# A gated feed-forward layer behind a spectral mixer: side work given out step by step between products

## The chip, the cores and the metric

The kernel runs on one core of one Trainium2 chip. The metric is the device time of one execution, in microseconds. Before the change three runs took 1896.96, 1904.18 and 1904.19 us; their median is 1904.18 us.

The engines have short names in the profile: PE is the matrix engine (PEld its weight loads), DVE the vector engine, ACT the scalar engine, POOL the general-purpose engine, SP the engine that issues most transfers. Each takes its instructions in the order in which the program gave them out, and waits at an instruction until what it needs is there.

## The reference

All is float32. There are 4096 positions of 640 channels. The first half normalises them, takes a real Fourier transform over the positions, passes the frequencies through two block-diagonal layers with a soft threshold, transforms back and adds the result to `x`. The second half normalises again and adds a gated feed-forward layer of 1728 hidden channels. Six vectors that come from `c` scale, shift and gate the two halves.

```python
mod = (_silu(c) @ w_mod).reshape(c.shape[0], 6, 1, -1)
sa, ca, ga, sb, cb, gb = ...
h = _layernorm(x) * (1 + ca) + sa
x = x + ga * _A_ref(h, A_w1, A_b1, A_w2, A_b2)      # spectral mixer
h = _layernorm(x) * (1 + cb) + sb
x = x + gb * ((_silu(h @ w_gate) * (h @ w_up)) @ w_down)
```

## The kernel before

The mixer fills the first 329 us and is not touched. The change lies in the second half, which runs from there to the end.

**Precision.** A float32 operand is split into a rounded high part and a low part, the rest (ACT copies the high part, DVE subtracts for the low part). A product is then three matmuls: high by high, high by low, low by high.

**Tiles.** The positions are 32 rows of 128. `TL` (L922) cuts them into six tiles t = 0 to 5 with 4, 6, 6, 6, 6 and 4 rows. Each tile goes through the same list of stages `STG`: `g0 u0 s g1 d0 u1 g2 d1 u2 g3 d2 u3 g4 d3 u4 g5 d4 u5 m d5`. A stage g, u or m multiplies the tile by 256 columns of the gate weights, of the up weights, or of 128 of both; s takes the last 64 columns of both. A stage d multiplies 256 hidden channels by the down weights and adds the result to `x`; d5 takes the rest of the hidden channels too.

- Tile 0 multiplies plainly (`plain`, L1293: 30 matmuls of 512 columns in a stage).
- Tiles 1 to 5 multiply two by two blocks with seven products in place of eight (`seven`, L1333: 54 matmuls of 384 columns, of 256 in tile 5). Four PSUM banks X, Y, Z, V gather the products. ACT copies a bank to SBUF at four moments (`keep`, L1360, tiles s_x, s_v, s_y, s_z), and the bank is then added to further. PE may go on in a bank when its copy is done. `done` (L1366) adds a bank to a copy (DVE), and makes SiLU (stage g) or multiplies by the gate and splits the result (stage u, m).
- `down` (L1435): 6 matmuls of 320 columns for each half of each row, and an addition on DVE.

**Side work.** Beside its products a tile has other work, done by ACT, DVE, POOL and SP, partly by PE:

- weights: load (`load_w`, L997), split (`prep_w`, L1017); in tile 0 also the block sums T1 to T4 of the seven products (`sum_w`, L1041: four POOL subtractions, two splits), which are stored to DRAM (`td`) and loaded again in each later tile (`load_t`, L1008). The place for them has two buffers, one for each half;
- down weights: load (`load_wd`), multiply by the gate vector on POOL (`fold_wd`, L1089), split (`split_wd`);
- the rows of the next tile: load (`row_load`), split (L1142, L1143), the last step of the inverse transform on PE (`row_dft`, L1152), residual and statistics on DVE, two small POOL steps, the normalised row (`row_norm`, L1164); for a pair of rows ten transposes on PE (`pair_turn`, L1177), scale and shift on ACT, four block sums on POOL, four splits, stores to DRAM (`hs`). The next tile loads all its pairs with `load_h` (L1228) at its start.

**The order around the change.** The program writes out the order by hand. `row_steps(t)` puts each of the row steps into a numbered stage: some at the stage's start, ahead of its products (the transform and the transposes), the others into a list `todo` with the weight steps. `fill()` is called six times in a stage and gives out a sixth of `todo`; the rest follows at the stage's end. Transfers for the next stages (`load_w`, `load_t`) are begun at the stage's start.

Of the kernel before, what the change touches and what calls it, by code (L numbers as in the profile page):

```python
# [171 lines left out]
def body(tc, x, w1, b1, w2, b2, wg, wu, wd, c, wm, k_fa, k_tb, k_tx, k_bm, k_bx, k_ga, k_ge, k_id, out, dbg=None):  # L172
# [27 lines left out]
    with ExitStack() as top:  # L200
# [716 lines left out]
        with ExitStack() as ff:  # L917
# [69 lines left out]
            def any_bank(name):  # L987
                nxt[0] += 1
                return bank((0, 1, 2, 3)[nxt[0] % 4], name)
# [7 lines left out]
            def load_w(t, n):  # L997
                k, p = WG[n]
                r = take("R", [P, 5, 256], F32, 2, f"r{t}_{n}")
# [8 lines left out]
            def load_t(t, n):  # L1008
                if WG[n][0] == "s":
                    return  # L1010
                for i in range(2):
                    wt = take("wt", [P, 2, 2, 2, P], F32R, 2, f"wt{t}_{n}{i}")
                    nc.sync.dma_start(f32(wt.rearrange("p a b c d -> p (a b c d)")), td[n, i])
                    wts[t, n, i] = wt


            def prep_w(t, n):  # L1017
# [12 lines left out]
                for ks in (slice(0, 2), slice(2, 5)):  # L1030
                    out += [lambda ks=ks: high(ks), lambda ks=ks: low(ks)]
                if c == P and t:

                    e, ks = slice(P, 2 * P), slice(0, 2)
                    out.insert(0, lambda: pool.tensor_tensor(r[:, ks, e], r[:, 1:4:2, 0:P], r[:, 0:4:2, 0:P],  # L1035
                                                             op=OP.subtract))
                    out += [lambda: high(ks, e), lambda: low(ks, e)]
# [3 lines left out]
            def sum_w(n):  # L1041
                r = raw[0, n]
                if WG[n][0] == "s":
                    return []
                ts = take(f"h{6 * (n % 2)}", [P, 4, 2, P], F32, 1, f"ts{n}")
# [3 lines left out]
                def sub(o, a, b):  # L1049
                    return lambda: pool.tensor_tensor(ts[:, o], a, b, op=OP.subtract)  # L1050

                out = [sub(3, b12, b11), sub(1, b22, ts[:, 3]), sub(0, b22, b12), sub(2, b21, ts[:, 1])]
                for i in range(2):
                    wt = take("wt", [P, 2, 2, 2, P], F32R, 2, f"wt0_{n}{i}")
                    wts[0, n, i] = wt
                    src = ts[:, 2 * i:2 * i + 2]

                    def high(wt=wt, src=src):
                        act.activation(wt[:, :, 0], src, AF.Copy)

                    def low(wt=wt, src=src):
                        dve.tensor_tensor(wt[:, :, 1], src, f32(wt[:, :, 0]), op=OP.subtract)

                    out += [high, low]
                return out

            def store_t(n):
                for i in range(2):
                    if (0, n, i) in wts:
                        nc.sync.dma_start(td[n, i], f32(wts[0, n, i].rearrange("p a b c d -> p (a b c d)")))  # L1070
# [3 lines left out]
            wds = {}  # L1074

# [10 lines left out]
            def fold_wd(t, p):  # L1086
                w = wdraw[t, p]
                for f in range(2):
                    pool.tensor_tensor(w[:, f], w[:, f], gbb, op=OP.mult)  # L1089

            def split_wd(t, p):
                w = wdraw[t, p]
                h = take("wdh", [P, 2, D], F32R, 2, f"wdh{t}_{p}")
                l = take("wdl", [P, 2, D], F32R, 2, f"wdl{t}_{p}")
                wds[t, p] = (h, l)
                out = []
                for f in range(2):
                    out += [lambda f=f: act.activation(h[:, f], w[:, f], AF.Copy),  # L1098
                            lambda f=f: dve.tensor_tensor(l[:, f], w[:, f], f32(h[:, f]), op=OP.subtract)]  # L1099
                return out  # L1100
# [15 lines left out]
            def gate_sum():  # L1116
                for hf in range(2):
                    pm = any_bank(f"gpm{hf}")
# [10 lines left out]
            hp_ = {}  # L1129

            def row_load(r):
# [3 lines left out]
                nc.sync.dma_start(crs[r], s2[:, r, :])  # L1135
                gtr[r] = fp.tile([P, 2, N1], F32R, tag="gt", bufs=2, name=f"gt{r}")
                pool.dma_start(gtr[r].rearrange("p b c -> p (b c)"), k_ga[:, 256 * r:256 * r + 256])

            def row_split(r):
                chh = take("pc", [P, D], F32R, 4, f"chh{r}")  # L1140
                chl = take("pc", [P, D], F32R, 4, f"chl{r}")
                act.activation(chh, crs[r], AF.Copy)  # L1142
                dve.tensor_tensor(chl, crs[r], f32(chh), op=OP.subtract)  # L1143
                chs[r] = (chh, chl)

            def row_dft(r):
                x2, gt = xr[r], gtr[r]
                chh, chl = chs[r]
                for hf in range(2):
                    e = slice(320 * hf, 320 * hf + 320)  # L1150
                    py = any_bank(f"py{r}_{hf}")
                    mm(py[:, :320], gt[:, 0, :], chh[:, e], start=True, stop=False)  # L1152
                    mm(py[:, :320], gt[:, 0, :], chl[:, e], start=False, stop=False)
                    mm(py[:, :320], gt[:, 1, :], chh[:, e], start=False, stop=True)
                    yg = take("s", [P, 320], F32, 5, f"yg{r}_{hf}")
                    dve.tensor_tensor(yg, py[:, :320], gab[:, e], op=OP.mult)
                    dve.tensor_tensor(x2[:, e], x2[:, e], yg, op=OP.add)
                mvs[r] = layer_stats(fp, x2.unsqueeze(1), 1, f"b{r}")

            def row_norm(r):  # L1160
                nc.sync.dma_start(x2d[:, r, :], xr[r])
                mv, rs = mvs[r]
                xn[r] = take("pc", [P, D], F32, 4, f"xn{r}")
                dve.tensor_scalar(xn[r], xr[r], mv[:, 0, 0:1], rs[:, 0:1], op0=OP.subtract, op1=OP.mult)  # L1164


            def pair_turn(t, i):
                r0, H = TL[t]
                rows = (r0 + i, r0 + H + i)
                h32 = take("h32", [P, 5, 2, P], F32, 1, f"h32_{t}_{i}")  # L1170
                hp_[t, i] = h32
                for q in range(3):
                    pt = any_bank(f"pt{t}_{i}_{q}")
                    for k in range(2 * q, min(2 * q + 2, 5)):
                        for a in range(2):
                            c = 256 * (k % 2) + 128 * a
                            pe.transpose(pt[:, c:c + 128], xn[rows[a]][:, 128 * k:128 * k + 128], idn)  # L1177
                    for k in range(2 * q, min(2 * q + 2, 5)):
                        c = 256 * (k % 2)
                        act.activation(h32[:, k].rearrange("p a b -> p (a b)"), pt[:, c:c + 256], AF.Identity,  # L1180
                                       bias=sb1[:, k:k + 1], scale=cb1[:, k:k + 1])


            def pair_parts(t, i):
                h32 = hp_[t, i]
                A = [[h32[:, b:4:2, a] for b in range(2)] for a in range(2)]
                sa_ = take("pc", [P, 2, 2, P], F32, 4, f"sa{t}_{i}")
                sb_ = take("pc", [P, 2, 2, P], F32, 4, f"sb{t}_{i}")
                S1, S2, S3, S4 = sa_[:, 0], sa_[:, 1], sb_[:, 0], sb_[:, 1]
                out = []  # L1190

                def tt(o, a, b, op):
                    return lambda: pool.tensor_tensor(o, a, b, op=op)

                out += [tt(S1, A[1][0], A[1][1], OP.add), tt(S3, A[0][0], A[1][0], OP.subtract),
                        tt(S2, S1, A[0][0], OP.subtract), tt(S4, A[0][1], S2, OP.subtract)]
                pieces = [[A[0][0], A[0][1]], [A[1][1], h32[:, 4]], [S1, S2], [S3, S4]]
                for j, src in enumerate(pieces):
                    ho = {}

                    def high(j=j, src=src, ho=ho):
                        o = fp.tile([P, 2, 2, 2, P], F32R, tag="ho", bufs=2, name=f"ho{t}_{i}_{j}")
                        ho[0] = o
                        for b in range(2):
                            act.activation(o[:, b, :, 0], src[b], AF.Copy)

                    def low(j=j, src=src, ho=ho):
                        o = ho[0]
                        for b in range(2):
                            dve.tensor_tensor(o[:, b, :, 1], src[b], f32(o[:, b, :, 0]), op=OP.subtract)  # L1210

                    def store(j=j, ho=ho):
                        nc.sync.dma_start(
                            hsd[t][:, 2 * j:2 * j + 2, :, :, 128 * i:128 * i + 128].rearrange(
                                "p a b c d -> p (a b c) d"),
                            f32(ho[0].rearrange("p a b c d -> p (a b c) d")))

# [400 lines left out]
```

## Time and profile before

| what | us |
|---|---|
| median of three runs | 1904.18 |
| profiled execution, its own time | 1901.75 |
| its span | 1900.0 |
| mixer, before the second half's first transposes | 329 |
| tile 0, to the start of d5; its d5 | 214.0; 28.8 |
| tile 1 | 298.1 |
| tile 2 | 286.7 |
| tile 3 | 286.0 |
| tile 4 | 265.7 |
| tile 5 | 191.7 |

The tiles are cut at the first matmul of their first stage. In a window's row the profile gives the time in which each engine was busy and, as PEclk, the share of full speed that the chip granted PE's clock. A row of waits reads: the waiting engine, what it was about to do, what it waited for, the sum in us, how often, the longest.

### The profile page before, as it was taken

To read this page: it belongs to the slowest core of one execution; us is meant where nothing else is said; L and a number is where in the kernel's file an instruction comes from. 1 tells how busy PE (TensorE), PEld (TensorE's weight loads), DVE (VectorE), ACT (ScalarE), POOL (GpSimd) and SP (SyncE) were. 2 spreads that over 40 slices of the span, in tenths; PEclk is the share of its full clock that TensorE was granted. 3 is DMA by queue.
4 is the path that set the end of the run, shared out by engine and by line. 5 is a ranking of instruction groups with operands and counts; after the bars stand their busy time and mean duration, and the time that the engine had idled before them with its cause. 6 is when DMAs were issued, how large, how long until landed. Compare 5 with 4: busy or idle time off the path is not lost.

```text
span 1900.0 us, 24357 instructions
## 1 busy us (share of the span) xinstructions
PE 1545.8 (81%) x8939; PEld 1443.1 (76%) x8939; DVE 1179.3 (62%) x2165; ACT 778.6 (41%) x1578; POOL 349.3 (18%) x433
## 2 busy tenths in 40 slices
PE   7699999777675877888877888877889788887778
PEld 3599997566565877788867888767879788887777
DVE  8578887656552665664665664665664666654665
ACT  7589884524232333342332342333342343323332
POOL 4301003344231021121021121021121021200111
PEclk9899999998887888999888999988899899999999
DMA  9745554635556563557553557553557545455442
GB/s 383 275 145 171 179 178 153 223 132 175 192 171 251 177 188 105 174 158 272 173 175 110 163 169 261 189 157 123 164 165 259 197 138 167 153 196 180 168 147 90
DMA packets 206680, 344.29 MB, mean 181 GB/s; under 512 B 20640, under 2 KB 136544, under 8 KB 204512
## 3 DMA queue, kind: packets, MB, share of 16 engines
q1 hardware_dynamic: 198336, 325.85, 51.7%
q0 software_dynamic: 6928, 14.91, 2.5%
q10 hardware_dynamic: 1296, 1.97, 0.3%
q8 instruction: 70, 1.15, 0.2%
q14 instruction: 50, 0.41, 0.1%
HBM read 249.88 MB, written 83.62 MB: 176 GB/s over the span
## 4 chain that ended last, share of the span: by engine, by line
PE 43%; DVE 22%; ACT 14%; DMA 10%; issue 6%; POOL 3%; SPq 2%; ACTq 0%; DVEq 0%; POOLq 0%
PE pd L1466 17%; PE pw L1350 5%; PE pw L1352 4%; PE pw L1351 4%; DVE wb L1028 4%; DVE sg L1380 3%; ACT a L1282 2%; DVE wdl L1099 2%; DVE a L1283 2%; DMA wdr<-in_B_w_down_dram 2%; ACT wb L1025 2%; PE pc L649 2%; DMA wt<-td 2%; DMA h<-hs 1%; DVE chl L1143 1%
## 5 line engine op out<-in xcount | busy, mean ns | idle before, releaser
L1466 PE MATMUL pd<-wdh,a 128*128 128x320 f32 x1712 | 398.5, 316 | 14.9 <-ACT wdh L1098 14.1
L1089 POOL TENSOR_TENSOR wdr<-wdr,gbb 128x640 f32<-128x640 f32 x84 | 142.1, 1710 | 1001.8 <-DMA wdr<-in_B_w_down_dram 751.0
L1466 PEld LDWEIGHTS pd<-wdh,a 128*128 128x128 f32 x1712 | 298.8, 194 | 16.5 <-ACT wdh L1098 15.1
L1350 PE MATMUL pw<-h,wt 128*128 128x384 f32 (+1 forms) x520 | 185.2, 356 | 119.1 <-ACT s_y L1362 68.6
L1466 PE MATMUL pd<-wdl,a 128*128 128x320 f32 x888 | 279.9, 316 | 2.5 <-DVE wdl L1099 2.1
L1028 DVE TENSOR_TENSOR wb<-r,wb 128x512 fp32r<-128x512 f32 (+3 forms) x173 | 160.4, 937 | 190.3 <-ACT wb L1025 183.4
L1470 DVE TENSOR_TENSOR x<-x,pd 128x320 f32<-128x320 f32 x384 | 180.7, 485 | 139.3 <-PE pd L1466 138.0
L1350 PEld LDWEIGHTS pw<-h,wt 128*128 128x128 f32 x520 | 104.7, 201 | 137.6 <-ACT s_y L1362 82.1
L1352 PE MATMUL pw<-h,wt 128*128 128x384 f32 (+1 forms) x520 | 177.5, 341 | 0.0
L1351 PE MATMUL pw<-h,wt 128*128 128x384 f32 (+1 forms) x520 | 177.0, 340 | 0.0
L1466 PEld LDWEIGHTS pd<-wdl,a 128*128 128x128 f32 x888 | 171.9, 194 | 5.6 <-DVE wdl L1099 5.5
L1362 ACT ACTIVATE s_x<-pw 128x384 f32<-128x384 f32 (+1 forms) x65 | 30.2, 465 | 328.0 <-PE pw L1352 328.0
L1282 ACT ACTIVATE a<-sg 128x384 fp32r<-128x384 f32 (+2 forms) x142 | 72.8, 512 | 216.8 <-DVE sg L1380 195.0
L1283 DVE TENSOR_TENSOR a<-sg,a 128x384 fp32r<-128x384 f32 (+2 forms) x142 | 93.7, 660 | 95.6 <-ACT a L1282 95.6
L1350 PE MATMUL pw<-h,wb 128*128 128x384 f32 (+1 forms) x390 | 140.2, 359 | 12.7 <-ACT wb L1025 11.9
L1352 PE MATMUL pw<-h,wb 128*128 128x384 f32 (+1 forms) x390 | 138.8, 356 | 2.7 <-DVE wb L1028 2.1
L1351 PE MATMUL pw<-h,wb 128*128 128x384 f32 (+1 forms) x390 | 137.2, 352 | 0.0
L1025 ACT ACTIVATE wb<-r 128x512 fp32r<-128x512 f32 (+3 forms) x173 | 115.5, 704 | 38.1 <-POOL r L1035 18.0
L1099 DVE TENSOR_TENSOR wdl<-wdr,wdh 128x640 fp32r<-128x640 f32 x84 | 70.2, 848 | 74.5 <-ACT wdh L1098 74.4
L1351 PEld LDWEIGHTS pw<-h,wt 128*128 128x128 f32 x520 | 105.3, 203 | 0.0
L1352 PEld LDWEIGHTS pw<-h,wt 128*128 128x128 f32 x520 | 104.5, 201 | 0.0
L1356 PE MATMUL pw<-h,wb 128*128 128x384 f32 (+1 forms) x260 | 88.5, 340 | 8.2 <-ACT s_z L1362 8.2
(252 smaller groups left out, 3331.0 us busy)
## 6 DMA issues: line engine op xcount, KB each, us to landing
wt<-td SPq DMA_DIRECT2D x130, 512.0 KB, 3.7
hs<-ho SPq DMA_DIRECT2D x56, 512.0 KB, 4.2
h<-hs SPq DMA_DIRECT2D x32, 768.0 KB, 11.3
r<-in_B_w_gate_dram SPq DMA_DIRECT2D x36, 640.0 KB, 6.0
r<-in_B_w_up_dram SPq DMA_DIRECT2D x36, 640.0 KB, 5.7
wdr<-in_B_w_down_dram SPq DMA_DIRECT2D x36, 640.0 KB, 5.7
td<-wt SPq DMA_DIRECT2D x25, 512.0 KB, 4.3
g<-s SPq DMA_DIRECT2D x28, 320.0 KB, 7.1
```

What stands on the lines that cost most here:

```text
L1025: act.activation(wb[:, 0, ks, e], r[:, ks, e], AF.Copy)
L1028: dve.tensor_tensor(wb[:, 1, ks, e], r[:, ks, e], f32(wb[:, 0, ks, e]), op=OP.subtract)
L1089: pool.tensor_tensor(w[:, f], w[:, f], gbb, op=OP.mult)
L1099: lambda f=f: dve.tensor_tensor(l[:, f], w[:, f], f32(h[:, f]), op=OP.subtract)]
L1282: act.activation(hi, a32, AF.Copy)
L1283: dve.tensor_tensor(lo, a32, f32(hi), op=OP.subtract)
L1350: mm(b, w(0, kp), a[:, kp, 0], start=start and kp == 0, stop=False, skip_group_check=not start)
L1351: mm(b, w(0, kp), a[:, kp, 1], start=False, stop=False, skip_group_check=not start)
L1352: mm(b, w(1, kp), a[:, kp, 0], start=False, stop=kp == 1, skip_group_check=not start)
L1356: mm(b, wb[:, 0, 4, c], AK[:, half, 0], start=False, stop=False, skip_group_check=True)
L1466: mm(pd[g, hf][:, :320], l, m, start=(i == 0), stop=(i == len(q) - 1))
L1470: dve.tensor_tensor(x2[:, e], x2[:, e], pd[g, hf][:, :320], op=OP.add)
```

## The change

The list `todo` and the numbered stages go. In their place stand six chains of single steps: `gate`, `prep` (weights), `down_w` (down weights), `sums`, `parts` (block sums of tile 0 and their splits) and `rows`. A step has an engine, a length in us, a function that gives out its instructions, and a pause until the next. The program keeps a count `now` of the time of PE's products and a count `free` for each engine. Every few matmuls it calls `slot`, which gives out those steps whose chain is due and whose engine is free by these counts; products' own work on ACT and DVE is added to the counts by `core`. Chains are emptied (`flush`) where their result is needed: `prep` at the end of a stage, `down_w` at the stage d that needs it, `rows` at d5.

Other edits: in `seven` the copies of the banks come first on ACT, the SiLU or high part of a quadrant follows after the next copy, the low part after that. `load_t` is called for each half where PE has given out the last product that reads the half's place, in place of both at the stage's start. In tile 0 weights are loaded three stages ahead, with a third buffer in a place (`h1`) that is empty until tile 1; g0's block sums and weights of tile 1 are fetched ahead of d5 instead of after it. Banks for side products are taken from three of the four bank names.

Each engine is given the same number of instructions by both kernels (PE 8672, DVE 2167, ACT 1589, POOL 438, SP 711); the order alone is another.

```diff
+            class Chain:
+                def add(self, steps, start=0.0):
+                    if not self.steps:
+                        self.ready = max(self.ready, now[0] + start)
+                    self.steps += steps
+                def run(self):
+                    e, n, f, pause = self.steps.pop(0)
+                    f()
+                    if e == "T":
+                        now[0] += n
+                        free[e] = now[0]
+                    else:
+                        free[e] = max(free[e], now[0]) + n
+                    self.ready = free[e] + pause
...
+            gate, prep, down_w, sums, parts, rows = chains = [Chain() for _ in range(6)]
+            def slot(n, hold=""):
+                now[0] += n
+                for c in chains:
+                    while c.steps and c.ready <= now[0] and free[c.steps[0][0]] <= now[0] + 0.2:
+                        if c.steps[0][0] in hold:
+                            break
+                        c.run()
...
+                return ([("A", 0.75, high, 0.1), ("V", 0.82, low, 0.3)],
+                        [("T", 0.45, lambda: dft(0), 0.0), ("T", 0.45, lambda: dft(1), 0.0),
+                         ("V", 1.0, lambda: residual(0), 0.0), ("V", 1.0, lambda: residual(1), 0.0),
+                         ("V", 1.2, stats, 0.1), ("S", 0.5, store, 1.4), ("V", 0.6, norm, 0.2)])
...
                 prod(V, S3, "T3", True)
                 s7 = keep(V, "v")
-                fill()
+                slot(2 * u)
                 prod(Y, A12, "B21", True)
                 fifth(Y, 0, 0)
-                fill()
-                done(0, 0, Y, s1)
+                summed(0, 0, Y, s1)
+                slot(1.5 * u)
+                slot(1.5 * u)
                 prod(X, S2, "T2")
-                s2_ = keep(X, "y")
-                fill()
+                sy = keep(X, "y")
+                high(0, 0, s1)
+                at(0)
+                slot(2 * u)
                 prod(V, A22, "T4")
                 fifth(V, 1, 0)
+                low(0, 0)
+                summed(1, 0, V, sy)
...
+                    if what == "d":
+                        while (t, NPR if n == NPR - 1 else n) not in wd_done:
+                            down_w.run()
+                        if n == NPR - 1:
+                            rows.flush()
+                            if t == 0:
+                                sums.flush()
+                                parts.flush()
+                                for i in range(2):
+                                    load_t(1, 0, i)
+                                prep.add(prep_w(1, 0))
+                            if t + 1 < NT:
+                                load_h(t + 1)
+                        down(t, n)
...
+                    if n == 2:
+                        if t == 0:
+                            prep_wd(0, 0)
+                            prep_wd(0, 1)
+                        else:
+                            load_x2(t)
+                        if t + 1 < NT:
+                            row_chain(t + 1)
```

More of the change, by code (lines that the diff above doesn't have):

```diff
@@ L1049, in sub @@
                 def sub(o, a, b):
[L1050 to L1070, printed above, removed]
+                    def f():
+                        if not ts:
+                            ts.append(take(f"h{6 * (n % 2)}", [P, 4, 2, P], F32, 1, f"ts{n}"))
+                        pool.tensor_tensor(ts[0][:, o], a if a is not None else ts[0][:, 3],
+                                           b if not isinstance(b, int) else ts[0][:, b], op=OP.subtract)
@@ L1176, in pair_turn @@
                             c = 256 * (k % 2) + 128 * a
-                            pe.transpose(pt[:, c:c + 128], xn[rows[a]][:, 128 * k:128 * k + 128], idn)
-                    for k in range(2 * q, min(2 * q + 2, 5)):
[L1179 to L1216, printed above, removed]
-                    out += [high, low, store]
-                return out
@@ new lines, in low, with store @@
+                def low(j):
+                    for b in range(2):
+                        dve.tensor_tensor(ho[j][:, b, :, 1], src(j)[b], f32(ho[j][:, b, :, 0]), op=OP.subtract)
+                def store(j):
+                    nc.sync.dma_start(
+                        hsd[t][:, 2 * j:2 * j + 2, :, :, 128 * i:128 * i + 128].rearrange("p a b c d -> p (a b c) d"),
+                        f32(ho[j].rearrange("p a b c d -> p (a b c) d")))
+                out = []
+                for q in range(3):
+                    out.append(("T", 0.1 * (4 if q < 2 else 2), lambda q=q: turn(q), 0.2))
+                    for k in range(2 * q, min(2 * q + 2, 5)):
+                        out.append(("A", 0.4, lambda k=k: scale(k), 0.0))
@@ L1221, in body, with pair_steps_at @@
+            def pair_steps_at(t, i, more):
+                st = pair_steps(t, i)
+                n = next(k for k, q in enumerate(st) if q[0] == "P")
+                return st[:n + 2] + more + st[n + 2:]
             hb = {}
@@ L1297, in plain @@
                     pg = first_g()
+                    for _ in range(8):
+                        slot(0.85)
                 else:
@@ L1400, in seven @@
-                fill()
+                sz = keep(X, "z")
+                high(1, 0, sy)
+                at(1)
+                slot(2 * u)
                 prod(Z, S4, "B22", True)
                 fifth(Z, 0, 1)
-                done(0, 1, Z, s3)
+                low(1, 0)
+                summed(0, 1, Z, sz)
+                slot(1.5 * u)
+                slot(1.5 * u)
                 fifth(X, 1, 1)
-                done(1, 1, X, s7)
-                fill()
-            def rest(t, n, fill):
+                summed(1, 1, X, s7)
@@ L1410, in rest @@
+                high(0, 1, sz)
+                low(0, 1)
+                high(1, 1, s7)
+                low(1, 1)
+                slot(u)
+            def rest(t, n):
                 N = P * TL[t][1]
```

433 lines of the change are left out of this document (240 added, 193 removed).

## The prediction

> **What bounds the kernel now.** I read the page's head first, then who waited for whom on PE in the second half, then the tiles as windows, then a few windows of 3.4 us for the clock.
>
> ```profile
> span 1900.0 us, 24357 instructions
> PE 1545.8 (81%) x8939; PEld 1443.1 (76%) x8939; DVE 1179.3 (62%) x2165; ACT 778.6 (41%) x1578; POOL 349.3 (18%) x433
> ```
>
> ```profile
> PE py L1152 <- ACT chh L1142: 86.0, 19, 12.3
> PE pw L1350 <- ACT s_y L1362: 68.6, 34, 6.3
> PE pt L1177 <- DVE xn L1164: 31.8, 8, 7.6
> PE pw L1350 <- DMA wt<-td: 30.2, 5, 17.4
> PE py L1153 <- DVE chl L1143: 22.3, 19, 3.4
> PE pw L1350 <- ACT s_x L1362: 19.6, 14, 2.8
> PE pd L1466 <- ACT wdh L1098: 14.1, 2, 13.1
> PE pw L1350 <- ACT wb L1025: 11.9, 8, 1.9
> PE pw L1356 <- ACT s_z L1362: 8.2, 3, 4.8
> ```
>
> ```profile
> 329.00:543.00 214.00, 159.66 (x739) 133.04 (x739) 130.25 (x213) 79.72 (x146) 81.38 (x92) 0.89 0.54 178
> 543.00:571.80 28.80, 15.08 (x87) 14.24 (x86) 13.63 (x22) 6.14 (x12) 8.03 (x10) 0.76 0.66 212
> 869.90:1156.60 286.70, 235.48 (x1293) 226.18 (x1292) 172.06 (x301) 96.34 (x196) 43.54 (x45) 0.90 0.54 176
> 1708.30:1900.00 191.70, 152.49 (x1061) 146.52 (x1060) 106.27 (x198) 64.17 (x149) 24.62 (x15) 0.94 0.44 145
> ```
>
> PE is the busiest engine, yet in the second half it waits some 310 us: 140 for the rows of the next tile (chh, chl, xn), 96 for bank copies on ACT (s_x, s_y, s_z), 30 for block sums from DRAM. No other engine is near full: in tile 2 DVE is busy 172 of 287 us.
>
> ```profile
> 1111.30:1114.70 3.40, 3.40 (x21) 3.26 (x19) 2.82 (x4) 2.49 (x4) 0.00 (x0) 1.00 0.12 23
> 1114.70:1118.10 3.40, 1.23 (x7) 1.05 (x7) 2.74 (x6) 0.90 (x2) 0.00 (x0) 1.00 0.34 131
> 1118.10:1121.50 3.40, 3.40 (x13) 3.40 (x12) 1.51 (x5) 1.51 (x4) 0.00 (x0) 0.50 0.56 181
> 1121.50:1124.90 3.40, 3.40 (x21) 3.40 (x20) 2.77 (x3) 0.53 (x1) 1.86 (x2) 1.00 1.05 320
> ```
>
> The second window has PE idle for 2.2 of 3.4 us; in the third the clock (last but two) is halved: 13 matmuls in place of 21. So a wait of 2 us costs 1.7 us more. The mean clock of the second half is 0.90, which is some 150 us of lost matmuls.
>
> **Floor.** Start to start at full clock a matmul of 384 columns takes 0.173 us (1135.15 to 1136.89: ten in 1.74), of 320 0.147, of 256 0.12, of 512 0.228. A tile of six rows: (13 x 54 + 30) x 0.173 + 492 x 0.147 + 12 for row transforms and transposes = 211 us, against 286.7. Tile 4 207, tile 5 136 (against 191.7), tile 0 up to d5 136, its d5 13.
>
> **The change part by part.**
>
> *Bank copies first.* Before, `done` put a high part on ACT, which waits for DVE, ahead of the copy that PE waits for. Now only the copy stands there. PE has 9 matmuls (1.56 us) between the end of a product in X and X's next use; a copy takes 0.49. What is late next: side steps on ACT just ahead of a copy (0.6 to 0.85 each), and high parts that wait for DVE. In the waits above copies and split weights together are 108 us, 22 for each of tiles 1 to 5; the least that can be left is 0. I take 12 for a tile of 384, 10 for tile 5: nearer the middle, as single steps still stand ahead of the copies. The half clock mostly goes with them, since a window needs well over a microsecond of waiting: I keep 5 a tile (4 in tile 4).
>
> *Transfers at the release.* `wt` is fetched where it was fetched in effect (SP waited there for PE); what stood behind it on SP no longer waits. But stages get shorter: from the last use of the first half to its next use are 33 matmuls, 5.7 us, where no d lies between (six times a tile), and a landing takes 3.1 to 9.7, median 3.7. Bounds 0 and 6 x 4 = 24; I take 9 a tile, 6 in tile 5, the median being inside.
>
> *Rows in a chain.* I walked the program's own counts, which fix the order and give no time. Of 138 row steps in a chain, 88 are still there when tile 0 reaches d5, 71 at tile 1's, 50 at tiles 2's and 3's; tile 4's shorter chain is empty. `rows.flush()` gives them out at once, ahead of the products of d5, and PE meets their transforms and transposes in order. So the 140 us of row waits inside the stages go, and a wait at d5 comes. Its links, from rows: split 0.83 (chl), 0.99 from there to the first residual step, residual 4 x 0.47, statistics 1.04, POOL and handovers 1.4, norm 0.61; the second row again 1.86 + 1.04 + 1.4 + 0.61. The second row's load is given out in the flush too and lands 4.8 us later. A whole pair (tiles 2, 3): 5.0 for DVE's backlog and the last splits, low part of the second row at 10.6, from there 1.04 + 1.4 + 0.61 + 4.9 = 8.0, so transposes at 18.8; less PE's own work 17. Tile 1 first finishes a pair: transposes at 4.2, scale 5 x 0.56, four pieces that share two places which a store frees after 5.1 us: next row split at 17.1, its pair done at 30.9; less PE's work 28. Tile 0 has two pairs: 15.7 + 26.7 = 42.4; less PE's work 37. The bounds: nothing if d5's matmuls were ahead of them (they are not), and half as much again if each load lands at 6.8 (its longest).
>
> *Start of the next tile.* `load_h` now stands on SP behind the last pair's stores, which end 17 us after the last transposes. Eight loads of 768 KB are 6.3 MB, 20 us at the 320 GB/s of the busiest window above. PE reaches its last use of them 28.4 us after the transposes (d5 19.4, 1.7 of half clock, most of 9.4): 6 us late at tiles 2, 3, 4. At tile 1 the stores of block sums and their loads stand ahead of it too (18.6), and d5 is 13: 17 us late. Before this wait was 0.8 in all.
>
> *Split weights.* By the program's counts DVE is still in the flush when tile 1 starts, so the splits of u0, s, g1 and u1 come only at the end of the stage before: a stage then waits for 0.63 + 0.69 + 0.84 + 0.95 and a handover, 3.8: 15 us. Tile 5, whose counts take the lengths of 384 columns, has the same three times, partly: 9. One down split at tile 1's d0: 4.
>
> *Tile 0.* To d5 now 214, floor 136. DVE has 130 us there, of which 22 move into the flush; so PE's floor stays ahead. g0 runs at half clock (30 matmuls in 10 us: 3 more), and 21 for loads and the gate sum (gate now 5.3, wb 3): 160. The turn: 37 + 13 + 2 half clock = 52.
>
> **Sum.** Tile 0 160 + 52. Tile 1: 211 + 17 (h) + 15 + 4 + 9 + 12 + 5 + 28 = 301. Tiles 2 and 3: 211 + 6 + 9 + 12 + 5 + 17 = 260 each. Tile 4: 207 + 6 + 9 + 12 + 4 = 238. Tile 5: 136 + 9 + 6 + 10 = 161. Together 1432 against 1571; with the mixer's 329 a span of 1761. The profiled execution is 1.75 us longer than its span and 2.4 below the median of the runs: **1765 us**.
>
> **A page's rule.** The rows first: the step chl takes 0.83 at the median and 2.15 at most, xn 0.61 and 1.86, which is 1.3 more, less than one POOL multiplication of 1.71. The Trainium skill, "SBUF — State Buffer", section on who interferes with whom, says that a DVE step with two SBUF inputs and a POOL step that reads SBUF hold one port in turn, so that the later one waits out the other; the rows agree, and the rule speaks against giving out POOL steps in the midst of the products. By it alone, if every one of a tile's 45 POOL steps met a DVE step that PE needs, a tile would be 58 us longer than my sum.
>
> ```profile
> L1143 DVE TENSOR_TENSOR chl<-cr,chh x28: 812/826/2154, 374.7 to 1596.9; 128x640 fp32r<-128x640 f32 x28
> L1164 DVE TENSOR_SCALAR xn<-x,mv_b,rs_b x28: 604/608/1864, 396.1 to 1614.3; 128x640 f32<-128x640 f32 x28
> L1089 POOL TENSOR_TENSOR wdr<-wdr,gbb 128x640 f32<-128x640 f32 x84 | 142.1, 1710 | 1001.8 <-DMA wdr<-in_B_w_down_dram 751.0
> ```
>
> **Rivals.**
>
> *A, less is lost than summed:* copies are never late and `wt` lands in time. 12 + 9 in each of tiles 1 to 4 and half the wait for h go: 1765 - 84 - 16 = about 1665 to 1700. For it: PE's 1.56 us against 0.49. Against it: DVE at 170 of 260.
>
> *B, side steps delay DVE and through it ACT and the copies.* DVE steps that are held up by POOL (1.3 us, as above) for a third of 45 steps a tile add 18 a tile, with tile 0's the same: 1765 + 95 = 1860.
>
> *C, slower:* the rows' PE steps stand in the midst of products now and wait for their rows there as they did at the stage's start, 140 us for 28 rows, and the flush comes on top: 1765 + 140 + 25 of half clock = 1930. It decides from 141 us on, 5 us a row. For it: 5 is what a row costs now. Against it: the chains leave pauses, and PE runs behind the counts, not ahead.
>
> *D, no change in sum:* flush waits and the loads for h come out twice as long as reckoned (99 + 35 more, as if each load and store on the way were waited for): 1765 + 134 = 1899, within half a per cent of now.
>
> **Chances and range.** Forecast 0.56 (its own range 1710 to 1825), A 0.18, B 0.14, C 0.08, D 0.04. The range that leaves out no more than 2 in 10 is 1675 to 1865, with A and B inside. Half a per cent, about what a measurement of this kernel tells from none, is 10 us: faster 0.88, same 0.03, slower 0.09.
>
> **What would show it.** Right: in the stages waits for s_y and chh near nothing and the clock at 1.00 there; PE idle ahead of each d5 but tile 4's and 5's, some 40, 30, 17 and 17 us, named after chl and xn; waits for h at four tiles' starts. Tile 2 at 260. Wrong: copies still waited for over 20 us a tile (B); L1152's successor waiting inside the stages (C); tiles 2 and 3 under 235 (A).

## The result, and the profile after

Four runs of the changed kernel took 1731.84 to 1738.24 us, with a median of 1734.76; four of the kernel before 1896.96 to 1908.23, with a median of 1904.18. The ratio is 0.9115, with a 95% interval from 0.9082 to 0.9147. The profiled execution took 1731.84 us, 1.74 more than its span.

The page of the changed kernel, its head:

```profile
span 1730.1 us, 24395 instructions
PE 1495.2 (86%) x8939; PEld 1406.3 (81%) x8939; DVE 1151.5 (67%) x2165; ACT 776.2 (45%) x1578; POOL 350.1 (20%) x433
```

PE is busy for 50 us less with the same 8939 matmuls, and 120 us of its idle time are gone. What PE waited for in the second half of the changed kernel (sum in us, times, longest):

```profile
PE py L1209 <- ACT chh L1198: 57.3, 10, 11.2
PE pt L1248 <- DVE xn L1226: 31.8, 12, 4.2
PE pw L1461 <- DMA wt<-td: 21.2, 5, 6.6
PE pw L1461 <- DMA h<-hs: 19.5, 11, 10.0
PE pd L1612 <- DVE wdl L1149: 14.8, 10, 3.6
PE pd L1612 <- ACT wdh L1145: 12.7, 6, 6.4
PE pw L1463 <- DVE wb L1075: 10.9, 9, 2.5
PE pw L1461 <- ACT wb L1072: 6.0, 3, 2.3
PE py L1209 <- DVE chl L1201: 3.8, 10, 0.8
PE pw L1461 <- ACT s_x L1473: 2.4, 3, 1.1
PE pw L1461 <- ACT s_y L1473: 2.2, 4, 0.6
```

Bank copies are down to 4.6 us, where they were 96. Waits for rows are down from 140 to 93, and they have moved: the windows below show where. In this view of the changed kernel the columns are the window and its length, the busy time of PE, PEld, DVE, ACT and POOL, PE's granted clock, the share of the transfer engines and GB/s.

```profile
329.00:482.00 153.00, 141.58 (x696) 119.01 (x692) 119.83 (x166) 68.60 (x121) 87.12 (x82) 0.97 0.65 214
482.00:528.20 46.20, 13.63 (x46) 9.65 (x45) 26.14 (x52) 10.96 (x23) 7.21 (x14) 0.56 0.50 151
825.50:1074.60 249.10, 219.66 (x1292) 214.15 (x1291) 163.96 (x301) 95.55 (x196) 43.09 (x45) 0.93 0.62 202
917.20:936.60 19.40, 19.40 (x116) 19.32 (x115) 14.60 (x24) 12.04 (x25) 6.08 (x6) 1.00 0.53 169
1028.80:1053.40 24.60, 8.22 (x30) 6.12 (x29) 14.06 (x31) 5.37 (x12) 1.58 (x4) 0.59 0.45 139
1550.90:1730.10 179.20, 150.59 (x1061) 145.30 (x1060) 97.39 (x198) 63.40 (x149) 22.33 (x15) 0.92 0.48 156
```

The rows are tile 0 to its flush, that flush, the whole of tile 2, two stages in the midst of tile 2, tile 2's flush ahead of d5, and tile 5. In the two stages, with rows and weights given out among the products, PE is busy for all of 19.40 us at full clock. In the two flushes it is busy for a third of the time, at a clock of 0.56 and 0.59.

| stretch | before | predicted | after |
|---|---|---|---|
| tile 0 to d5 or its flush | 214.0 | 160 | 153.0 |
| flush and d5 of tile 0, and tile 1 | 326.9 | 353 | 343.5 |
| tile 2 | 286.7 | 260 | 249.1 |
| tile 3 | 286.0 | 260 | 249.1 |
| tile 4 | 265.7 | 238 | 227.2 |
| tile 5 | 191.7 | 161 | 179.2 |
| sum | 1571 | 1432 | 1401 |

So the gain lies in tile 0 (61 us), tiles 2 to 4 (about 38 each) and tile 5 (12). Around tile 0's turn 17 us are given back.

### The profile page after: what moved, and what is told of

Read it like the earlier page. It is cut to its first block, busy times and chain, and to the rows that moved or that the text cites. A ratio compares the mean times of both kernels' runs of the same rounds, so it can differ in the third digit from the quotient of the medians.

```text
span 1730.1 us, 24395 instructions
## 1 busy us (share of the span) xinstructions
PE 1495.2 (86%) x8939; PEld 1406.3 (81%) x8939; DVE 1151.5 (67%) x2165; ACT 776.2 (45%) x1578; POOL 350.1 (20%) x433
## 5 line engine op out<-in xcount | busy, mean ns | idle before, releaser
L1612 PE MATMUL pd<-wdh,a 128*128 128x320 f32 x1712 | 406.7, 318 | 12.7 <-ACT wdh L1145 12.7
L1612 PEld LDWEIGHTS pd<-wdh,a 128*128 128x128 f32 x1712 | 302.1, 195 | 14.7 <-ACT wdh L1145 14.5
L1461 PE MATMUL pw<-h,wt 128*128 128x384 f32 (+1 forms) x520 | 176.0, 338 | 32.0 <-DMA wt<-td 21.2
L1075 DVE TENSOR_TENSOR wb<-r,wb 128x512 fp32r<-128x512 f32 (+3 forms) x173 | 148.8, 863 | 45.8 <-ACT wb L1072 41.9
L1462 PE MATMUL pw<-h,wt 128*128 128x384 f32 (+1 forms) x520 | 172.1, 331 | 0.0
L1463 PE MATMUL pw<-h,wt 128*128 128x384 f32 (+1 forms) x520 | 172.0, 331 | 0.0
L1461 PE MATMUL pw<-h,wb 128*128 128x384 f32 (+1 forms) x390 | 130.8, 335 | 19.4 <-DMA h<-hs 13.4
L1463 PE MATMUL pw<-h,wb 128*128 128x384 f32 (+1 forms) x390 | 131.4, 337 | 11.3 <-DVE wb L1075 10.9
L1461 PEld LDWEIGHTS pw<-h,wt 128*128 128x128 f32 x520 | 100.6, 193 | 39.8 <-DMA wt<-td 22.6
L1462 PE MATMUL pw<-h,wb 128*128 128x384 f32 (+1 forms) x390 | 129.9, 333 | 0.0
L1072 ACT ACTIVATE wb<-r 128x512 fp32r<-128x512 f32 (+3 forms) x173 | 120.2, 702 | 0.2 <-DMA r<-in_B_w_gate_dram 0.2
L1482 DVE TENSOR_TENSOR s_x<-pw,s_x 128x384 f32<-128x384 f32 (+1 forms) x65 | 34.5, 530 | 109.8 <-PE pw L1469 100.9
L1499 ACT ACTIVATE a<-sg 128x384 fp32r<-128x384 f32 (+1 forms) x130 | 65.1, 501 | 90.4 <-DVE sg L1494 90.4
L1463 PEld LDWEIGHTS pw<-h,wt 128*128 128x128 f32 x520 | 100.8, 194 | 0.0
L1462 PEld LDWEIGHTS pw<-h,wt 128*128 128x128 f32 x520 | 100.8, 194 | 0.0
L1461 PEld LDWEIGHTS pw<-h,wb 128*128 128x128 f32 x390 | 76.2, 196 | 21.8 <-issue 10.3
L1463 PEld LDWEIGHTS pw<-h,wb 128*128 128x128 f32 x390 | 76.1, 195 | 16.1 <-DVE wb L1075 16.1
## 6 DMA issues: line engine op xcount, KB each, us to landing
h<-hs SPq DMA_DIRECT2D x32, 768.0 KB, 11.4
```

The costliest lines, as they stand in the source:

```text
L1072: act.activation(wb[:, 0, ks, e], r[:, ks, e], AF.Copy)
L1075: dve.tensor_tensor(wb[:, 1, ks, e], r[:, ks, e], f32(wb[:, 0, ks, e]), op=OP.subtract)
L1461: mm(b, w(0, kp), a[:, kp, 0], start=start and kp == 0, stop=False, skip_group_check=not start)
L1462: mm(b, w(0, kp), a[:, kp, 1], start=False, stop=False, skip_group_check=not start)
L1463: mm(b, w(1, kp), a[:, kp, 0], start=False, stop=kp == 1, skip_group_check=not start)
L1482: dve.tensor_tensor(s, b, s, op=OP.add)
```

## Experiments

The theory ahead of the runs was that of the prediction: the new order in a stage takes away the copy waits, the chains take the row waits out of the stages, and the flush at d5 gives part of that back. Each run below stands beside seven runs of the kernel before on the same chip, with medians of 1906.83, 1904.85 and 1904.2 us in the three groups.

### The order of the copies undone (copies_undone)

```diff
-                sy = keep(X, "y")
                 high(0, 0, s1)
+                sy = keep(X, "y")
...
-                sz = keep(X, "z")
                 high(1, 0, sy)
+                sz = keep(X, "z")
```

> The changed kernel with one edit taken back: in a stage of seven products the SiLU or high part of a quadrant stands ahead of the next bank copy on ACT again. Theory (the order of the copies is worth what the waits for s_y, s_x and s_z were before, 96 us, and the half clock after them): those waits come back to 50 to 96 us, and the time is 1800 to 1850 us. Rival (the chains alone keep DVE in time, so the order no longer matters): under 15 us more, 1735 to 1750 us.

Measured: 1743.56 us, ratio 0.9149 (0.9114 to 0.9184). The median is 9 us above the changed kernel's, and the intervals overlap: the rival held. The theory that the order of the copies is needed fell. What ACT waits for, in the run with the order undone:

```profile
ACT a L1499 <- DVE sg L1494: 167.9, 130, 4.2
```

and in the changed kernel:

```profile
ACT a L1499 <- DVE sg L1494: 90.4, 82, 2.5
```

ACT does stand for 77 us more at high parts that wait for DVE, with copies behind them. PE hardly notices. In the list of PE's waits of the run with the order undone, copies have 10.2 us in all, where the changed kernel has 4.6:

```profile
PE pw L1467 <- ACT s_z L1473: 8.1, 10, 2.1
PE pw L1461 <- ACT s_y L1473: 2.1, 3, 0.9
```

ACT's own waits for PE ahead of the copies s_y and s_z fell at the same time, from 64.0 and 78.0 us to 6.5 and 2.5: the wait for DVE mostly takes the place of a wait for the product that ACT would have had anyway, and most copies still end before PE comes back to the bank.

### The order of the copies alone (copies_alone)

The kernel before, with `todo` and `fill` as they were, and only the order inside `seven` changed:

```diff
                 fifth(Y, 0, 0)
                 fill()
-                done(0, 0, Y, s1)
+                summed(0, 0, Y, s1)
                 prod(X, S2, "T2")
-                s2_ = keep(X, "y")
+                sy = keep(X, "y")
+                high(0, 0, s1)
                 fill()
...
+                low(0, 0)
```

> The kernel before with this one edit alone: copies first in the stages of seven products, the list todo and the numbered stages as they were. Theory: the 96 us of waits for copies fall to some 20, half-clock time falls with them, row waits (140 us) stay: 1790 to 1830 us. Rival (copies were late because a sixth of todo stood in front of them, so the order alone does nothing): 1880 to 1905 us.

Measured: 1813.31 us, ratio 0.9507 (0.9464 to 0.9551), inside the theory's range, but only in part by the waits that it named. PE's waits in this run:

```profile
PE py L1152 <- ACT chh L1142: 75.3, 19, 11.8
PE pt L1177 <- DVE xn L1164: 27.0, 8, 5.4
PE pw L1356 <- ACT s_z L1362: 21.6, 12, 4.9
PE pw L1350 <- ACT s_x L1362: 18.2, 8, 4.6
PE py L1153 <- DVE chl L1143: 10.1, 19, 2.3
```

Of 96 us of copy waits 42 stay (21.6, 18.2 and 2.2 for s_y), twice the 20 expected, and the waits for rows, expected to stay at 140, fall to 112; why they fall, no run shows. The two parts aren't additive: the order alone is worth 93 us, the rest of the change with the old order 163, both together 170. The order alone takes away over half of the copy waits, the rest of the change nine tenths.

### The release of the places undone (release_undone)

```diff
+                at(0)
+                at(1)
                 prod(X, A11, "B11", True)
...
-                at(0)
                 slot(2 * u)
...
-                at(1)
                 slot(2 * u)
```

> The changed kernel, with the two loads of block sums given to SP at the start of the stage before, as in the kernel before. SP then stands waiting for PE until the fourth and sixth product, with the stage's side loads and stores behind it. Theory (the load starts at the same moment either way; side transfers come up to 7 us later, which the pauses mostly cover): 3 to 20 us more, 1738 to 1755 us. Rival (this is a main part of the gain): 40 us more or above. Rival (no part of it): within 3 us.

Measured: 1752.86 us, ratio 0.9186 (0.914 to 0.9232), 18 us more than the changed kernel, inside the expected range. By the ratios it is 13.5 us, and the two intervals just overlap, so the size is uncertain. The cost does not come as a wait for transfers: the waits for `wt` are 13.2 us, where the changed kernel has 21.2. PE's largest new wait in this run:

```profile
PE pw L1461 <- ACT s_y L1473: 15.8, 19, 2.2
```

and what ACT waits for there:

```profile
ACT wdh L1145 <- POOL wdr L1140: 81.4, 35, 7.7
```

In the changed kernel the same row of ACT has 20.9 us, and PE's waits for s_y have 2.2. One case in tile 2 shows the way. With the wait for a place back at the stage's start, SP gives out the load of the down weights at 895.46, behind the two loads of `wt` from 892.45 (in the changed kernel it is given out at 882.69, ahead of those of 891.34). POOL, which waited for it, multiplies from 900.86, and ACT stands at the split that needs this, with the bank copy behind it:

```profile
902.45 0.74 ACT L1145 ACTIVATE wdh<-wdr 128x640 fp32r<-128x640 f32 x1 [1.78 <-POOL wdr L1140]
903.10 0.47 ACT L1473 ACTIVATE s_y<-pw 128x384 f32<-128x384 f32 x1
```

PE waits 0.28 us for that copy, up to 903.62. A wait on SP for a place thus reaches PE over three engines.

### Counts brought up to date after the flush (sync)

A flush adds the steps' lengths to `free`, but not to `now`, so that the program takes DVE and ACT for busy well into the next tile. One line sets `now` behind the flush:

```diff
                                 load_h(t + 1)
+                            now[0] = max(now[0], free["V"], free["A"])
                         down(t, n)
```

> The changed kernel, with one line more: after the rows are given out at d5, the count now is set to the counts of DVE and ACT, so that the program knows that PE has waited. Row steps left at d5: 88, 50, 50, 50 instead of 88, 71, 50, 50. Theory: tile 1 loses its waits for split weights (7 us) and the down split (4), and its wait at d5 falls from 25 to 17 us as in tile 2: 12 to 22 us less, 1713 to 1723 us. Rival (the waits in tile 1 come from late h loads and stay): within 5 us of 1735.

Measured: 1713.11 us, ratio 0.8991 (0.896 to 0.9022). Tile 1, whose flush waited 15.1 for chh and 9.2 for xn in the changed kernel, now has tile 2's waits for rows and split weights:

```profile
PE py L1209 <- ACT chh L1198: 10.3, 2, 6.0
PE pt L1248 <- DVE xn L1226: 5.0, 2, 4.0
PE pw L1463 <- DVE wb L1075: 3.5, 2, 2.5
```

Tile 1's waits for split down weights are gone from the list too, while its wait for h stays (14.5 us for 13.8) and one of 5.5 for `wt` comes. So 22 us of the changed kernel's time were due to the program's counts, not to work.

### Lengths by the tile's width (scale)

```diff
-                    core("A", 0.49)
+                    core("A", 0.49 * N / 384)
...
-                    core("V", 0.55)
+                    core("V", 0.55 * N / 384)
```

> The changed kernel, with the lengths that the products' own work adds to the counts of DVE and ACT taken for the tile's width (256 columns in tile 5, not 384). At tile 5's stages d no down split is then left over. Theory (the 19 us of waits for wdh and wdl in tile 5 and the half clock after them come from the counts): 20 to 35 us less, 1700 to 1715 us. Rival (DVE is truly full in tile 5: 97 us busy of 179, 136 at PE's floor, so the splits are late whatever the counts): within 8 us of 1735.

Measured: 1711.93 us, ratio 0.8973 (0.8945 to 0.9). Tile 5 of the changed kernel waited for split down weights:

```profile
PE pd L1612 <- ACT wdh L1145: 11.4, 5, 6.4
PE pd L1612 <- DVE wdl L1149: 8.0, 7, 3.4
```

and with the lengths scaled:

```profile
PE pd L1612 <- ACT wdh L1145: 3.7, 1, 3.7
PE pd L1612 <- DVE wdl L1149: 0.7, 1, 0.7
```

Tile 5 then takes 157.9 us, where it took 179.2. Its banks have 256 columns. With the lengths of 384 the program takes ACT and DVE to be busier than they are, and leaves the down splits to the moment when they are needed.

### Rival B: POOL's work taken out (no_fold)

```diff
-                    pool.tensor_tensor(w[:, f], w[:, f], gbb, op=OP.mult)
+                    if t == 0:
+                        pool.tensor_tensor(w[:, f], w[:, f], gbb, op=OP.mult)
```

> The changed kernel without the multiplication of the down weights by the gate vector in tiles 1 to 5 (that part of the result is left out): 120 us less work on POOL. Theory (nothing that PE waits for hangs on POOL in the stages): within 5 us of 1735. Rival (DVE steps held up by POOL delay ACT and through it PE): 20 to 60 us less, and DVE's busy time falls.

Measured: 1730.2 us, ratio 0.9069 (0.9033 to 0.9105), which overlaps the changed kernel's interval. The low part of a row, with its least, median and longest duration in ns, in the changed kernel:

```profile
L1201 DVE TENSOR_TENSOR chl<-cr,chh x28: 812/819/2244, 376.2 to 1469.2; 128x640 fp32r<-128x640 f32 x28
```

and without POOL's multiplications:

```profile
L1202 DVE TENSOR_TENSOR chl<-cr,chh x28: 812/818/826, 378.3 to 1464.5; 128x640 fp32r<-128x640 f32 x28
```

The delay of DVE by POOL is real: without that work on POOL the longest is 0.83 us instead of 2.24, and DVE is busy for 157.25 us in tile 2 instead of 163.96. It costs PE nothing that can be measured; DVE has 85 us of idle time in that tile.

### One tile's rows held back for the flush (hold_rows)

The chain of rows is held in tile 3 until d5, which then finds three pairs to do in place of one:

```diff
+                held[0] = t == 3
...
                 for c in chains:
+                    if c is rows and held[0]:
+                        continue
```

> The changed kernel, with the rows' chain held back in tile 3 alone until d5, so that all three pairs are given out there at once instead of the last one. Theory (each pair in the flush costs PE its whole chain, some 26 us, which no product covers): PE's wait ahead of that d5 grows from 17 to some 65 to 70 us, and the time by 45 to 60 us less the 4 to 8 us that the rows took inside the stages: 1775 to 1795 us. Rival (the wait is DVE's backlog at the end of stage m, and further pairs run in its shadow): under 25 us more.

Measured: 1798.2 us, ratio 0.9424 (0.9373 to 0.9474), 63 more than the changed kernel, a little over the range. Two windows of it, a pair of tile 3's stages that now have no rows among them, and the flush:

```profile
1248.40:1267.10 18.70, 18.70 (x109) 18.47 (x107) 12.96 (x22) 10.07 (x20) 0.00 (x0) 1.00 0.43 132
1267.10:1339.80 72.70, 21.39 (x68) 15.55 (x67) 38.48 (x76) 16.32 (x37) 12.84 (x24) 0.52 0.49 151
```

The stages without rows are shorter by 0.70 us than tile 2's with them, which is no more than the seven matmuls that they lack: the rows cost no wait there. The flush is 72.7 us where tile 2's is 24.6, so 24 a pair; 51 us of it are waits of PE, fewer than the 65 to 70 expected, and the mean clock in it is 0.52. Tile 3's stages ahead of the flush are 8 us shorter than in the changed kernel, of which the two pairs' own matmuls are some 5 (24 at 0.147 and 20 at 0.09). The excess lies behind the flush. Tile 4 is 8 us longer (stage s 8.1 for 5.3, d0 17.4 for 11.4, where splits come late as in tile 1 of the changed kernel), and tile 5's first two stages take 27.2 us for 15.2, with a wait of 8.1 for `wt` among them; why tile 5 is hit, no run shows. This prices the place of a row's steps: no wait seen among the products, 12 us a row at d5.

### Output stores behind the loads (outs_late)

At the start of tile 3 SP issues, in the changed kernel (start, length in us):

```profile
1063.94 8.29 SPq L1327 DMA_DIRECT2D h<-hs  x8
1072.33 9.69 SPq L1623 DMA_DIRECT2D out_dram<-x  x6
...
1087.86 1.90 SPq L1060 DMA_DIRECT2D wt<-td  x2
```

and the transfers of that stretch, from 1062 to 1096, come to

```profile
DMA packets 6488, 11.88 MB, mean 349 GB/s; under 512 B 1625, under 2 KB 4183, under 8 KB 6487
```

So the one large wait for `wt` in a tile (5.6 us, up to 1095.22) comes behind eight loads, and behind six stores that nobody waits for. SP itself stood at these stores: 7.3 us of their 9.69 it waited behind the loads of h. The edit keeps the stores of tiles 0 to 4 in a list and begins them in g0 of the next tile, behind the second `load_t`:

```diff
-                            (nc.scalar if t == NT - 1 else nc.sync).dma_start(ov[:, TL[t][0] + g, :], x_row(t, g))
+                            nc.scalar.dma_start(ov[:, TL[t][0] + g, :], x_row(t, g))
+                        elif last and t < NT - 1:
+                            outs.append((t, g))
...
                     def at(i):
...
+                        while i and n == 0 and outs:
+                            q, g = outs.pop(0)
+                            nc.sync.dma_start(ov[:, TL[q][0] + g, :], x_row(q, g))
```

> The changed kernel, with the six stores of the output of tiles 0 to 4 given to SP in stage g0 of the next tile behind the second load of block sums, in place of between d5's products. From 1062 to 1094 us of the changed kernel's trace the transfer engines are full (93 to 104%), and the stores (2 MB, about 6 us at 345 GB/s) stand ahead of the block sums that PE waits 5.6 to 6.6 us for at u0. Theory (that wait is bandwidth, taken by the stores): the waits for wt fall from 21 us to under 8, waits for h fall a little, 15 to 30 us less with the half clock: 1705 to 1720 us. Rival (the loads of h alone fill it): within 6 us of 1735.

Measured: 1711.42 us, ratio 0.8994 (0.8964 to 0.9025), as expected. PE's wait for `wt` in this run, 21.2 in the changed kernel:

```profile
PE pw L1461 <- DMA wt<-td: 3.6, 4, 1.0
```

That the stores make the wait is shown; that they do it through bandwidth, as expected, is not. The transfer engines are as full around this tile's start as before (371 GB/s from 1055 to 1089), but SP gives out the loads of `wt` 6.6 us after the tile's first product, where it was 13.3.

### Together (best, best_outs)

`best` has sync and scale, the rows first among the chains, begun at the tile's first stage, and a backlog of 0.8 us allowed on an engine:

```diff
-            gate, prep, down_w, sums, parts, rows = chains = [Chain() for _ in range(6)]
+            gate, rows, prep, down_w, sums, parts = chains = [Chain() for _ in range(6)]
...
-                    while c.steps and c.ready <= now[0] and free[c.steps[0][0]] <= now[0] + 0.2:
+                    while c.steps and c.ready <= now[0] and free[c.steps[0][0]] <= now[0] + 0.8:
...
-                        if t + 1 < NT:
+                    if n == (0 if t else 2) and t + 1 < NT:
                             row_chain(t + 1)
```

> The changed kernel with counts set right after the flush, lengths by the tile's width, the rows' chain looked at before the weights' chain and begun at stage g0 of tiles 1 to 3, and 0.8 us in place of 0.2 as the backlog that an engine may have. Row steps left at d5: 58, 10, 10, 10 and none; the ten left have no PE step among them. Theory (the waits at d5 are the rows' steps on PE): the waits ahead of d5 fall from 33, 25, 17, 17 us to about 20, 0, 0, 0, tile 5 gains as in the run with the lengths, and some of it is lost to weights split later: 1620 to 1655 us. Rival (the rows then delay split weights in the stages by as much): 1690 us or more.

Measured: 1642.22 us, ratio 0.8605 (0.8574 to 0.8637). `best_outs` has the late stores as well:

> The run best with the same edit. Theory: waits for wt fall from 29 to under 8 us: 1612 to 1630 us. Rival: within 5 us of 1642.

Measured: 1617.69 us, ratio 0.849 (0.8449 to 0.8531), 6.7% below the changed kernel and inside the range, though the waits for `wt` fell from 29.1 to 11.4 us and not under 8. PE's waits in the second half of `best_outs`:

```profile
PE pw L1461 <- DMA h<-hs: 17.1, 8, 10.6
PE py L1209 <- ACT chh L1198: 16.6, 2, 11.1
PE pw L1463 <- DVE wb L1075: 15.4, 7, 2.7
PE pw L1461 <- ACT s_x L1473: 11.8, 16, 1.4
PE pw L1461 <- DMA wt<-td: 11.4, 4, 3.8
```

With rows first, the flushes of tiles 1 to 3 have nothing for PE to wait for: the 16.6 for chh lie wholly in tile 0's, and 12.4 of the 17.1 for h right behind it. Copies are waited for somewhat more (11.8 for s_x); the larger backlog may be the price, but no run changes the backlog alone.

## Why the prediction was right, and where it was off

The forecast was the right mechanism: row waits out of the stages, a smaller wait at d5, copies no longer late. Its sum was 31 us too high, from terms of both signs: copies, `wt` and h together came out 90 us below what was reckoned, half clock and tile 5's down splits 58 above. That the sum is nearer than its terms is in part luck.

- **Bank copies, 12 a tile kept: mis-sized.** They measured 4.6 us in all five tiles, not 58. The step that failed is "nearer the middle, as single steps still stand ahead of the copies". The order alone leaves 42 us and the rest of the change alone 10, as the two runs on the order show, and together there is almost nothing. The lower end of the bound was the value to take.
- **wt, 9 a tile over six places: the wrong place.** The six gaps of 5.7 us inside a tile are long enough. The wait is 5.6 to 6.6 us once in tiles 2 to 4, at u0, behind the loads and stores of the tile's start. The prediction had put `load_h` on SP there, and left out the output stores that stand behind it; the run with late stores shows that they make the wait. The five tiles together have 21.2 us, where 42 were reckoned.
- **Rows: right.** Among the products no waits of PE for rows are left in tiles 1 to 4. The flush waits were 32.6, 24.8, 16.3 and 16.7 us at tiles 0 to 3, where 37, 28, 17 and 17 were reckoned, and nothing at tile 4. A pair held back costs 24 us; the prediction's difference between one pair and two was 26.7. One of its links is misread: 5.1 us is the median landing of stores to and loads from `hs` taken together, and the stores alone have 4.2 before the change and 3.5 after.
- **h, 17 and three times 6: too high.** Measured 13.8, 2.1, 2.6 and 1.0. The 320 GB/s taken from the busiest window before was too low a rate: while the loads run, windows of the changed kernel show some 410 GB/s, at which 6.3 MB would take 15 us and not 20 (an estimate).
- **Split weights.** Tile 1: 10.6 (wb 7.0, wdl 3.6), reckoned 19. In tiles 2 to 4 3.4 each were left, and 2.8 for a down split in tile 4, reckoned none. Tile 5: 3.8 for gate and up weights, reckoned 9.
- **Tile 5's down splits: a missed term.** They cost 19.4 us of waits, and half clock after them, for which tile 5's sum had no term. The prediction saw that tile 5's counts "take the lengths of 384 columns" and drew it for the gate and up splits alone; the same counts starve the down splits too. Tile 5 is the only stretch that came out above its sum, 179.2 for 161, and the run with scaled lengths takes the cause away.
- **Half clock, 5 a tile: too low.** In tile 2 PE was busy for 219.7 where the floor is 211: 8.7 us. Reckoned so, tiles 1 to 5 lost 19.6, 8.7, 8.9, 5.4 and 14.6 us, 57 in all, where the sum had 19. Tile 2 then adds up: 219.7, 16.3 of flush, 5.9 wt, 3.4 split weights, 2.1 h, 1.5 copies make 248.9 of 249.1.
- **Tile 0: 153.0 for 160**, and its turn with tile 1 343.5 for 353.

*The rivals.* A was half right: copies were hardly ever late, but `wt` was, and tile 5 took back 18 us. B's mechanism exists and costs nothing that can be measured, as the run without POOL's multiplications shows; its 18 us a tile would be 19.5 by its own factors (1.3 for a third of 45). By the Trainium skill, "SBUF — State Buffer", section on who interferes with whom, the delay by POOL of a DVE step with two SBUF inputs was to be expected; the two rows of chl agree with it. The prediction counted xn as agreeing too, but that step has one tensor as input, and the rule as told there does not cover it. The 58 us a tile that the prediction worked out from it as the worst did not come, as the run without POOL's multiplications gained nothing that can be measured. C did not come: PE had no waits for row steps among the products of tiles 1 to 4, and a row at d5 costs 12 us, as hold_rows shows. D asked for waits at the flush and for h twice as long as the 99 and 35 us reckoned; they came to 90 and 20.

Left open: the turn at tile 0. Two pairs are still done there in the best kernel, and no run here tried to begin tile 1's rows inside the mixer.

## What to carry to other kernels

Side work given out one step at a time among the products can go without a wait, while the same steps behind a barrier cost their whole chain of latencies, here 24 us for a pair of rows. So the chain that ends in a barrier should go first, not last; the best kernels do so, together with other edits. Where a program orders work by its own counts of time, each place where the counts part from the machine (after a flush, for a narrower tile) is worth looking up: two such places cost 22 and 23 us here. When a transfer that is waited for stands behind stores that nobody waits for on the same queue, move the stores (23 us here).

## What the runs showed that was not expected

**PE's clock falls and rises by different bounds.** The clock's records change at boundaries 3.41 us apart. Cut at these, in the second half of the changed kernel, the shortest idle time that a window at full clock was followed by half clock with is 1.55 us, and the longest still followed by full clock 1.83. A window at half clock went back to full with up to 0.55 us of idle time, and stayed at half from 0.71 on. In the kernel before, the same four figures are 1.59, 1.67, 0.59 and 0.36, so that neither bound is sharp in these cuts. Two stretches of the changed kernel, one at tile 3's start:

```profile
1077.70:1081.11 3.41, 2.22 (x11) 1.48 (x9) 1.42 (x2) 0.41 (x1) 0.00 (x0) 1.00 1.04 404
1081.11:1084.53 3.42, 1.96 (x11) 1.64 (x11) 0.56 (x1) 0.90 (x2) 0.00 (x0) 1.00 0.97 340
1084.53:1087.94 3.41, 2.89 (x16) 2.57 (x17) 0.00 (x0) 0.90 (x2) 0.00 (x0) 1.00 1.04 401
```

and one in tile 1:

```profile
610.07:613.48 3.41, 0.53 (x4) 0.24 (x2) 2.63 (x5) 2.40 (x4) 0.00 (x0) 1.00 0.26 102
613.48:616.90 3.42, 2.71 (x10) 2.71 (x11) 1.88 (x3) 0.00 (x0) 0.00 (x0) 0.50 0.23 37
616.90:620.31 3.41, 3.41 (x15) 3.41 (x14) 0.97 (x2) 0.00 (x0) 1.17 (x1) 0.50 1.05 381
```

In the first, idle times of 1.19, 1.46 and 0.52 us leave the clock at 1.00. In the second, one window with 2.9 us idle halves it, and 0.71 us in the next keep it at half for a third, though PE is busy for all of that. A wait of 2 us that falls into one such window thus costs 1.7 more, but a second short one right behind it costs that again. The time at half clock in the second half fell from 311 us before to 229 in the changed kernel and 106 in `best`.

**At the start of a tile the transfer engines are full.** The last columns of the first three rows above show it, at 340 to 404 GB/s; the mean share over a tile (0.62 in tile 2) doesn't tell it. The order of the transfers then decides whether PE waits: the run with late stores has the engines as full there, and hardly a wait for `wt`.
